# Joining the small TensorE runs of a fused attention, routing and gated-FFN kernel

## The chip, the cores and the metric

The kernel runs on one core of a Trainium2 chip. The metric is the time of one execution on the device in microseconds. Five engines work side by side, each through its own list of instructions in order: TensorE (PE: products), VectorE (DVE), ScalarE (ACT), GpSimd (POOL) and SyncE (SP, which issues most DMAs). Semaphores tie the lists together.

## The reference

Three layers follow one another, for 4 batches of 576 tokens:

```python
# 1 attention over 32 memory slots, 8 heads of 64
a = exp(phi - max_s(phi));  a = a / (sum_s(a) + 1e-9)           # over the 576 tokens
k_m, v_m = a^T k, a^T v                                          # 32 x 64 per head
attn = softmax(q k_m^T / 8);  x = attn v_m                       # heads side by side: 512 wide
# 2 one expert of 8 per token
logits = x w_gate;  gate = sigmoid(x w_local)
e[s] = argmax(logits[s]) if s == 0 or gate[s] < 0.5 else e[s-1]
x = softmax(logits)[e] * (relu(x w1[e]) w2[e])                   # 512 -> 1024 -> 512
# 3 gated FFN
h = relu(x w_in);  out = (h * sigmoid(conv3(h))) w_out           # conv over tokens, per channel
```

With these inputs each batch keeps the expert of its first token. The kernel computes all tokens of a batch with that expert and, at the end, looks whether another one is needed.

## The kernel before, in words

A float32 product is made of three products of rounded halves (high and low parts), 128x128 weights by 288 columns: half of the tokens. These are the plain products. For a batch `b` the list `order()` (line 58) writes 24 steps out: `h` eight times (hidden layer of the expert for one half of the tokens, 6 plain products each), `y` four times (second layer, 24 plain products each), then the same for the other half. Behind the steps it names what is done for later batches: `c = b + 1` and `d = b + 2`. Batch 0 has its own list, `FIRST` (line 51), whose steps 0 to 11 lie in `OPENING` (line 40).

The expert's first layer is not applied to x. V w1 is computed first (`vw`, tile `pv`: the memory values times a head's rows of w1, four quarters of w1, two quarters per PSUM tile), and the slot weights `att` multiply it.

The side work on TensorE, with the names of its PSUM tiles: phi's transposes (`pback`, `pa`), the memory products (`mem`, `pk`), the memory transposed (`back`, `pkt`), the gate weights (`gatew`, `pw`: memory values times w_gate and w_local, 9 columns, copied by ScalarE into `vwg`, line 475), the scores of half the tokens (`scores`, `sc`), the first token's logits (`flog`, `pfc`, from which VectorE takes the expert), the logits of all tokens of two batches (`rtok`, `pl`), and at the end of routing the transposes `pt` and `pp` and two tiny products, `pe` (`rown`, line 684) and `pf` (`close`, line 710). Scores, gate weights and V w1 use tiles of 64 rows by 32 columns of the array, eight at a time.

The scores go through VectorE's transpose (`scores_back`, line 489), maximum, difference, ScalarE's exponential, sum, reciprocal, product, and a second transpose. ScalarE and VectorE also evict each plain product: `h` by both (lines 781 and 782), `y` by ScalarE (line 864). They split the raw pieces of w2 into high and low parts (lines 147 and 148), and convert the words of the float64 weights of layer 3 (`nar`, lines 213 to 218).

PSUM has 8 banks. `bank()` takes one of four single banks (plain products, `pk`, `pl`, `pfc`, `pkt`, `pe`, `pf`). `banks()` takes one of two double banks (`pa`, `sc`, `pw`, `pv`, `pt`, `pp`); whoever comes third waits until the first one's reader is done.

TensorE's order is the written list. In the opening those of VectorE, ScalarE and SyncE are written too. In the 24-step part a planner orders them when the kernel is built: by its own model of times, among the instructions that are ready then, by place in the list. Instructions under `urgent()` count as 1500 places earlier. The lists are fixed when the kernel runs.

Of the kernel before, what the change touches and what calls it, by code (L numbers as in the profile page):

```python
# [8 lines left out]
F32 = mybir.dt.float32  # L9
# [5 lines left out]
ALU = mybir.AluOpType  # L15
AX = mybir.AxisListType
# [18 lines left out]
def units(b):  # L35
# [8 lines left out]
strn.0.0 smx.0.0 ssub.0.0 sexp.0.0 ssum.0.0 warm.1.8 mem.2.0 mem.2.1 warm.1.1 w1.0 q.0.1 wload.0.0 wload.0.1 kv.3 vwe.0 vwh.0 warm.1.2 vwe.1 ahi.0.0 vwh.1 alo.0.0 vwl.0 vwl.1 warm.1.3 wload.0.2  # L44
q.1.0 wload.0.3 q.1.1 cload nload.0 nload.1 phi.4 kv.4 prec.2 memf.2 pmax.3
h.0 vw.0.1 h.0 pexp.3 vw.0.2 h.0 prec.3 h.0 w2part.0 vw.0.3 h.0 scores.0.1 strn.0.1 w2part.1 h.0 pback.3 h.0 h.0 smx.0.1 w2.0.1 ssub.0.1 w2.0.2 sexp.0.1
y.0 firstq.2 phi.5 kv.5 mem.3 ssum.0.1 w2.0.3 y.0 back.1 ahi.0.1 alo.0.1 nar.0 nload.2 y.0 gatew.1 frow.1 fexp.1 nar.1 nload.3 y.0
""".split()


FIRST = {
# [3 lines left out]
}  # L55


def order():


    words = [4]

    def each(c, *parts):
        return [f"{part}.{u}" for u in units(c) for part in parts] if c < B else []

    def of(c, *parts):
        return [f"{part}.{c}" for part in parts] if c < B else []

    def narrow_next():
        i = words[0]  # L70
        words[0] += 1
        return [f"nar.{i}"] + [f"nload.{i + 2}"] * (i < 14)

    out = []
    for b in range(B):
        c, d = b + 1, b + 2
        whole = c < B
        after = {i: [] for i in range(24)}
        if b == 0:
            for i, more in FIRST.items():  # L80
                after[i] += more.split()
        else:
            for i, more in {
                1: of(c, "frow", "fexp") + [f"save.{b}"],
                2: [f"w2.{b}.2"] + [f"rtok.{b // 2}"] * (b == 1) + of(d, "firstq") + each(d, "phi", "kv"),
                3: [f"scores.{c}.0", f"ssoft.{c}.0"] * whole,
                7: [f"w2.{b}.3"],
                8: [f"scores.{c}.1", f"ssoft.{c}.1"] * whole + each(d, "psoft"),
                9: of(c, "flog", "w1"),
                10: each(d, "pback"),  # L90
                12: [f"asplit.{c}.0", f"asplit.{c}.1"] * whole,
                13: each(d, "mem"),
                16: of(d, "back"),
                18: of(d, "gatew"),
                21: [f"vw.{c}.0", f"vw.{c}.1", f"w2.{c}.0"] * whole,
                22: [f"vw.{c}.2", f"vw.{c}.3", f"w2.{c}.1"] * whole,
                23: [f"q.{d}.0", f"q.{d}.1"] * (d < B),
            }.items():
                after[i] += more
            for i in ((), (6, 13, 15, 17, 19), (4, 7, 13, 15, 17, 19), (8, ))[b]:  # L100
                after[i] += narrow_next()
            if not whole:
                for i, more in {0: "rtok.1 rback rall", 8: "rpp", 9: "rown", 10: "close yload.0 win.0 win.1",
                                19: "ysplit.0", 20: "win.2 win.3"}.items():
                    after[i] += more.split()
        for i in range(0 if b else 12, 24):
            out += [f"h.{b}" if i % 12 < 8 else f"y.{b}"] + after[i]
    assert words[0] == 16
    return out
# [5 lines left out]
def fused_kernel(tc, q, first, first_q, kv, kv_tail, phi, w1, w2, w_in, conv_w, w_out, out):  # L115
    nc = tc.nc
    wide = w_in.dtype == I64
    PSUM = bass.MemoryType.PSUM
    with (
# [8 lines left out]
        def bank(name):  # L128
            return ps1.tile([128, 512], F32, tag="one", name=name)
# [60 lines left out]
        nc.gpsimd.memset(first2, 0.0)  # L190
        code0 = const.tile([1, 4], F32, name="code0")
        convw = const.tile([128, 3, 8], F32, name="convw")
        fx = const.tile([32, 1], F32, name="fx")
        code32 = const.tile([1, 32], F32, name="code32")
        e0i = const.tile([1, B, 8], U32, name="e0i")
        flf = const.tile([1, 32], F32, name="flf")
        fli = const.tile([1, 32], I32, name="fli")
        ones = const.tile([8, 128], F32, name="ones")
        nc.vector.memset(ones, 1.0)
# [289 lines left out]
        def scores_back(b, hf):  # L489

            sts[b, hf] = work(f"st{b}_{hf}")
            nc.vector.transpose(two(sts[b, hf]), scs.pop((b, hf))[:, :, :HALF])
# [27 lines left out]
                cols = slice(32 * hs.start, 32 * hs.stop)  # L520
                nc.vector.transpose(attf[b, hf].rearrange("p g t -> p (g t)")[:, cols], st[:, cols])

        def slot_top(b, hf):
            scores_back(b, hf)
            slot_max(b, hf)
            slot_difference(b, hf)

        def slot_softmax(b, hf):

            slot_top(b, hf)  # L530
            slot_exp(b, hf)
            slot_weights(b, hf)

# [77 lines left out]
        def route_all():  # L611

            lg = routes[0].rearrange("p b c n -> p (b c) n")
            room = ap.tile([128, S], F32, tag="ph", bufs=2, name="room")
            pack = ap.tile([128, S], F32, tag="ph", bufs=2, name="pack")[:96, :384].rearrange("p (c n) -> p c n", n=64)
            packs.append(pack)
            used = [0]

            def bc(t):
                return t.rearrange("p (c o) -> p c o", o=1).to_broadcast([96, 24, 8])  # L620

            def by_batch(t):
                return t.rearrange("p (b c) n -> p b c n", b=B)

            def packed(at):
                return pack[:, :, at:at + 32].rearrange("p c (b n) -> p b c n", n=8)

            def tile24(name, *n):
                n = n[0] if n else 0
                at = used[0]  # L630
                used[0] += 24 * max(n, 1)
                t = room[:96, at:used[0]]
                return t.rearrange("p (c n) -> p c n", n=n) if n else t

            l8 = lg[:, :, 0:8]
            mx = tile24("rmx")
            nc.vector.reduce_max(mx, l8, axis=AX.X)
            eq = tile24("req", 8)
            nc.vector.tensor_tensor(eq, l8, bc(mx), ALU.is_ge)
            nc.vector.tensor_tensor(eq, eq, codes, ALU.mult)  # L640
            cd = tile24("rcd")
            nc.vector.reduce_max(cd, eq, axis=AX.X)
            ex = tile24("rex", 8)
            nc.vector.tensor_tensor(ex, l8, bc(mx), ALU.subtract)
            nc.scalar.activation(ex, ex, AF.Exp)
            gf = tile24("rgf", 1)
            nc.vector.tensor_scalar(gf, lg[:, :, 8:9], GATE_SHUT, None, ALU.is_le)
            nc.vector.memset(by_batch(gf)[0:1, :, 0:1, :], 1.0)
            nc.vector.tensor_tensor(cd, cd, gf.rearrange("p c o -> p (c o)"), ALU.mult)
            nc.vector.tensor_copy(packed(0), by_batch(bc(cd)))  # L650
            sm = tile24("rsm")
            nc.vector.reduce_sum(sm, ex, axis=AX.X)
            nc.vector.tensor_scalar(sm, sm, EPS, None, ALU.add)
            nc.vector.reciprocal(sm, sm)
            nc.vector.tensor_tensor(packed(32), by_batch(ex), by_batch(bc(sm)), ALU.mult)
            nc.vector.tensor_copy(code32.rearrange("p (b n) -> p b n", n=8),
                                  code0.rearrange("p (b o) -> p b o", o=1).to_broadcast([1, B, 8]))

        def route_scan():
# [20 lines left out]
        def route_first():  # L680

            act, = acts
            pe = bank("pe")
            nc.tensor.matmul(pe[:32, 0:1], code32, ones[0:1, 0:1], start=True, stop=True)
            oh = ap.tile([32, 1], F32, tag="oh", name="oh")
            nc.vector.tensor_tensor(oh, pe[:32, 0:1], code_e, ALU.is_equal)
            nc.vector.tensor_scalar(act, act, 0.0, None, ALU.is_gt)
            nc.vector.tensor_tensor(fx, act, oh, ALU.subtract)

        def attention_high(b, hf):  # L690
            if hf == 0:
# [14 lines left out]
            attention_low(b, hf)  # L706

        def route_last():
            pf = bank("pf")
            nc.tensor.matmul(pf[0:1, 0:32], fx, ident[:32, :32], start=True, stop=True)  # L710
            nc.vector.tensor_copy(flf, pf[0:1, 0:32])
            nc.vector.reduce_sum(anyf, flf, axis=AX.X)
            nc.vector.tensor_copy(fli, flf)
            nc.vector.tensor_copy(anyi, anyf)

        att, e0 = {}, {}
# [190 lines left out]
        def gated_w(kc):  # L907
# [4 lines left out]
            "phi": load_phi, "kv": load_kv, "q": load_q,  # L912
            "gates": load_gates, "psoft": phi_softmax, "pback": phi_back,
            "mem": memory, "memf": memory_out, "warm": warm, "back": memory_back,
            "scores": scores, "gatew": gate_weights, "firstq": first_queries, "frow": first_row, "fexp": first_weights, "flog": first_expert, "ssoft": slot_softmax,
            "pmax": phi_max, "pexp": phi_exp, "prec": phi_sums, "smax": slot_top, "strn": scores_back, "smx": slot_max,
            "ssub": slot_difference, "sexp": slot_exp, "ssum": slot_weights, "ahi": attention_high, "alo": attention_low,
            "rtok": route_tokens, "save": save, "rback": route_back, "rall": route_all, "rpp": route_scan, "rown": route_first, "asplit": split_attention,
            "vwe": first_vw, "vwh": first_vw_high, "vwl": first_vw_low, "vw": expert_vw, "w2": expert_w2, "nload": load_words, "nar": narrow, "win": gated_w,
# [230 lines left out]
```

## Time and profile before

| | us |
|---|---|
| median of 3 timed runs (417.91 to 418.92) | 418.08 |
| profiled execution | 417.01 |
| its span | 415.2 |
| TensorE busy in the span | 406.6 (98%) |
| VectorE, ScalarE, POOL busy | 276.3, 222.0, 74.6 |

The granted clock of TensorE has a mean of 0.997 of full speed. The gated FFN takes the span from 209 us to the end; what the change touches on TensorE lies between 44 and 190 us. The chain that ended last goes back from the last instruction to what released it, or to the instruction before it on its engine. Ends of products are modelled, and starts of small products overlap, so what a run costs is best read from where the next run begins.

### The profile page before, as it was taken

The page shows a single profiled execution, that of the slowest core. Times are in us where ns is not written, and L with a number is a line of the kernel's source. Part 1 is how long each engine was busy: PE and PEld are TensorE (multiplying, and loading weights), DVE is VectorE, ACT ScalarE, POOL GpSimd, SP SyncE. Part 2 cuts the span into 40 slices and gives each one's busy share as a digit, 9 for nine tenths or more (in the row PEclk, how much of TensorE's full clock was granted, in tenths as well). Part 3 has the DMA queues.
Part 4 walks back from the last instruction along what each step waited for, and adds up shares of the span by engine and source line. Part 5 has one row for each costly group of instructions (what it writes and reads, how often), then busy time and mean ns, then how long its engine had stood idle before and what let it go on. Part 6 is the DMA issues. An engine that isn't in the chain of part 4 may idle for free.

```text
span 415.2 us, 8514 instructions
## 1 busy us (share of the span) xinstructions
PE 406.6 (98%) x3406; PEld 370.6 (89%) x3407; DVE 276.3 (67%) x509; ACT 222.0 (53%) x414; POOL 74.6 (18%) x121
## 2 busy tenths in 40 slices
PE   8999999999999999999999999999999999999994
PEld 7779988989989998899999988998889988999884
DVE  3689899695777974966979980688105792178500
ACT  4366577455657264645848742677215772277320
POOL 1000202311122211311101620034100332014300
PEclk9999999999999999999999999999999999999998
DMA  8999989967892699946640032000120000100022
GB/s 288 343 403 401 340 305 363 410 220 277 303 310 93 200 366 407 340 157 186 194 152 0 2 114 103 0 2 0 57 70 2 0 2 29 72 2 2 2 77 57
DMA packets 23904, 69.04 MB, mean 166 GB/s; under 512 B 3280, under 2 KB 4048, under 8 KB 23856
## 3 DMA queue, kind: packets, MB, share of 16 engines
q1 hardware_dynamic: 20272, 56.88, 39.1%
q0 software_dynamic: 3584, 11.54, 7.1%
q8 instruction: 28, 0.46, 0.5%
q14 instruction: 20, 0.16, 0.1%
HBM read 52.08 MB, written 16.33 MB: 165 GB/s over the span
## 4 chain that ended last, share of the span: by engine, by line
PE 96%; ACT 1%; DMA 1%; DVE 1%; issue 0%; ACTq 0%
PE py L160 25%; PE pi L160 24%; PE po L1058 24%; PE ph L160 12%; PE pv L455 2%; PE pk L412 2%; PE idle L462 2%; PE sc L455 1%; PE pa L390 1%; DMA ph<-in_phi 1%; PE pl L593 1%; PE pk L402 0%; DVE wb L148 0%; PE pkt L446 0%; ACT wb L147 0%
## 5 line engine op out<-in xcount | busy, mean ns | idle before, releaser
L160 PE MATMUL py<-h,wb 128*128 128x288 f32 x768 | 108.2, 298 | 0.0
L160 PEld LDWEIGHTS py<-h,wb 128*128 128x128 f32 x768 | 103.0, 188 | 4.2 <-issue 3.4
L160 PE MATMUL pi<-yh,wi 128*128 128x288 f32 x512 | 90.4, 295 | 0.0
L1058 PE MATMUL po<-wo,g 128*128 128x512 f32 (+1 forms) x408 | 90.2, 377 | 0.0
L1058 PEld LDWEIGHTS po<-wo,g 128*128 128x128 f32 x408 | 72.8, 188 | 13.2
L160 PEld LDWEIGHTS pi<-yh,wi 128*128 128x128 f32 x512 | 76.3, 188 | 0.9
L1040 DVE SCALAR_TENSOR_TENSOR ct<-ht,convw,ct 128x575 f32<-128x575 f32 x32 | 31.0, 968 | 52.1 <-ACT ct L1039 52.1
L160 PE MATMUL pi<-yl,wi 128*128 128x288 f32 x256 | 54.6, 295 | 0.0
L160 PE MATMUL ph<-att,vh 128*128 128x288 f32 x256 | 53.5, 302 | 0.3 <-DVE h L782 0.3
L1023 POOL CAST tail<-g 128x128 fp32r<-128x128 f32 x32 | 23.0, 723 | 122.9 <-DVE g L148 122.3
L160 PEld LDWEIGHTS ph<-att,vh 128*128 128x128 f32 x256 | 40.6, 188 | 4.6 <-DVE h L782 1.7
L865 POOL DMA_DIRECT2D ydram<-ys x32 | 17.4, 545 | 146.7 <-ACT ys L864 140.3
L160 PEld LDWEIGHTS pi<-yl,wi 128*128 128x128 f32 x256 | 41.1, 188 | 0.0
L1037 ACT ACTIVATE ht<-pi 128x576 f32<-128x576 f32 x32 | 20.8, 651 | 33.5 <-PE pi L160 33.5
L160 PE MATMUL ph<-att,vl 128*128 128x288 f32 x128 | 37.7, 296 | 0.0
L782 DVE SCALAR_TENSOR_TENSOR h<-ph,h 128x288 fp32r<-128x288 f32 x64 | 28.1, 449 | 12.8 <-ACT h L781 12.7
L781 ACT ACTIVATE h<-ph 128x288 fp32r<-128x288 f32 x64 | 25.7, 408 | 16.5 <-PE ph L160 16.1
L864 ACT ACTIVATE ys<-py 128x288 f32<-128x288 f32 x32 | 13.1, 408 | 37.5 <-PE py L160 25.2
L1082 ACT ACTIVATE ot<-po 128x512 f32<-128x512 f32 x17 | 9.5, 598 | 43.3 <-PE po L1058 43.3
L1018 DVE TENSOR_TENSOR ct<-ht,ct 128x576 f32<-128x576 f32 x32 | 27.0, 844 | 7.2 <-ACT ct L1017 7.1
L1042 DVE SCALAR_TENSOR_TENSOR ct<-ht,convw,ct 128x575 f32<-128x575 f32 x32 | 28.3, 886 | 0.4
L147 ACT ACTIVATE g<-ct 128x576 fp32r<-128x576 f32 x32 | 21.7, 681 | 12.6 <-DVE ct L1018 12.6
(234 smaller groups left out, 505.2 us busy)
## 6 DMA issues: line engine op xcount, KB each, us to landing
kv<-in_kv SPq DMA_DIRECT2D x16, 512.0 KB, 8.5
q<-in_q SPq DMA_DIRECT2D x8, 576.0 KB, 10.3
ydram<-ys POOLq DMA_DIRECT2D x32, 144.0 KB, 5.3
y<-ydram SPq DMA_DIRECT2D x4, 1152.0 KB, 6.8
out<-ot SPq DMA_DIRECT2D x15, 256.0 KB, 2.0
ph<-in_phi SPq DMA_DIRECT2D x8, 288.0 KB, 7.3
adram<-at POOLq DMA_DIRECT2D x8, 288.0 KB, 7.7
wa_1r<-in_w SPq DMA_DIRECT2D x4, 512.0 KB, 4.5
```

The source lines that it names most:

```text
L147: pin(nc.scalar.activation(hi, src, AF.Copy))
L160: pin(nc.tensor.matmul(ps, st, mv[:, cols], start=i == 0, stop=i == len(terms) - 1))
L781: nc.scalar.activation(t[:, 0, :], ps, AF.Relu)
L782: low = nc.vector.scalar_tensor_tensor(t[:, 1, :], ps, 0.0, t[:, 0, :].bitcast(F32), ALU.max, ALU.subtract)
L864: nc.scalar.activation(yt, ps, AF.Copy)
L865: stored.append(nc.gpsimd.dma_start(ydram[b, d, :, half(hf)], yt).ins)
L1018: slow(f"gm.{f}").tensor_tensor(ct, ht, ct, ALU.mult)
L1023: nc.gpsimd.tensor_copy(tail[:, f, :, to:to + 64], t[:, :, 512:576].bitcast(F32))
L1037: nc.scalar.activation(two(ht), halves(ps), AF.Relu)
L1040: nc.vector.scalar_tensor_tensor(ct[:, 1:], ht[:, :S - 1], convw[:, 0, f:f + 1], ct[:, 1:], ALU.mult, ALU.add)
L1042: nc.vector.scalar_tensor_tensor(ct[:, :S - 1], ht[:, 1:], convw[:, 2, f:f + 1], ct[:, :S - 1], ALU.mult, ALU.add)
L1058: nc.tensor.matmul(ps[:, cols], st[sp], w[:, mp, f % 2, cols], start=f == 0 and i == 0, stop=f == 7 and i == 2)
```

## The change

In the written list the side work moves together. In batch 0 the gate weights of batch 1 leave the opening and come at step 12, ahead of both halves' scores and of the first token's product; the second scores no longer stand at step 16. The two memory products stand together at step 19, and all four quarters of V w1 with the gate weights at step 21. In the later batches the logits, both halves' scores and the first token's product stand at step 3 (before: steps 2, 3, 8 and 9), and the gate weights (before: step 18) and all quarters of V w1 (before: steps 21 and 22) at step 21. The transposes of both halves' scores are listed right behind the scores; the rest of the softmax (`sweigh`) stays at steps 3 and 8.

The products `pe` and `pf`, which turned a row into a column and back, become VectorE transposes of 32x32 tiles; the tiles `fx`, `code32` and `flf` grow to 32x32, and POOL clears two of them at the start.

```diff
-y.0 ... nload.2 y.0 gatew.1 frow.1 fexp.1 nar.1 nload.3 y.0
+y.0 ... nload.2 y.0 frow.1 fexp.1 nar.1 nload.3 y.0
-    12: "scores.1.0 flog.1 w1.1 psoft.4", 13: "ssoft.1.0 psoft.5", 16: "pback.4 scores.1.1 ssoft.1.1", 17: "pback.5",
-    18: "mem.4", 19: "mem.5 nar.2 nload.4", 20: "asplit.1.0 asplit.1.1 back.2",
-    21: "gatew.2 vw.1.0 vw.1.1 w2.1.0 nar.3 nload.5", 22: "vw.1.2 vw.1.3 w2.1.1 conv", 23: "q.2.0 q.2.1 save.0",
+    12: "gatew.1 scores.1.0 scores.1.1 flog.1 w1.1 strn.1.0 strn.1.1 psoft.4", 13: "sweigh.1.0 psoft.5", 16: "pback.4 sweigh.1.1",
+    17: "pback.5", 19: "mem.4 mem.5 nar.2 nload.4", 20: "asplit.1.0 asplit.1.1 back.2",
+    21: "gatew.2 vw.1.0 vw.1.1 vw.1.2 vw.1.3 w2.1.0 nar.3 nload.5", 22: "w2.1.1 conv", 23: "q.2.0 q.2.1 save.0",
...
-                2: [f"w2.{b}.2"] + [f"rtok.{b // 2}"] * (b == 1) + of(d, "firstq") + each(d, "phi", "kv"),
-                3: [f"scores.{c}.0", f"ssoft.{c}.0"] * whole,
+                2: [f"w2.{b}.2"] + of(d, "firstq") + each(d, "phi", "kv"),
+                3: [f"rtok.{b // 2}"] * (b == 1) + [f"{item}.{c}.{hf}" for item in ("scores", "strn") for hf in range(2)] * whole
+                   + of(c, "flog") + [f"sweigh.{c}.0"] * whole,
-                8: [f"scores.{c}.1", f"ssoft.{c}.1"] * whole + each(d, "psoft"),
-                9: of(c, "flog", "w1"),
+                8: [f"sweigh.{c}.1"] * whole + each(d, "psoft"),
+                9: of(c, "w1"),
-                18: of(d, "gatew"),
-                21: [f"vw.{c}.0", f"vw.{c}.1", f"w2.{c}.0"] * whole,
-                22: [f"vw.{c}.2", f"vw.{c}.3", f"w2.{c}.1"] * whole,
+                21: of(d, "gatew") + [f"vw.{c}.{q}" for q in range(4)] * whole + [f"w2.{c}.0"] * whole,
+                22: [f"w2.{c}.1"] * whole,
...
-            pe = bank("pe")
-            nc.tensor.matmul(pe[:32, 0:1], code32, ones[0:1, 0:1], start=True, stop=True)
+            nc.vector.transpose(code_t, code32)
...
-            pf = bank("pf")
-            nc.tensor.matmul(pf[0:1, 0:32], fx, ident[:32, :32], start=True, stop=True)
-            nc.vector.tensor_copy(flf, pf[0:1, 0:32])
-            nc.vector.reduce_sum(anyf, flf, axis=AX.X)
-            nc.vector.tensor_copy(fli, flf)
+            nc.vector.transpose(flf, fx)
+            nc.vector.reduce_sum(anyf, flf[0:1, :], axis=AX.X)
+            nc.vector.tensor_copy(fli, flf[0:1, :])
```

## Rows read from the trace of the kernel before

**Rows 1.** The page, part 4: shares of the chain that ended last, by engine.

```profile
PE 96%; ACT 1%; DMA 1%; DVE 1%; issue 0%; ACTq 0%
```

**Rows 2.** The chain in order of time: start us, us, engine, tile, line, count.

```profile
83.78 2.94 PE py L160 x22
...
86.73 0.53 PE py L160 x2
...
107.93 0.20 PE pw L455 x13
108.13 1.01 PE ph L160 x6
...
115.51 1.02 PE pv L455 x32
116.53 3.40 PE py L160 x24
...
127.48 0.65 PE sc L455 x16
...
131.48 3.20 PE py L160 x24
...
183.03 0.15 PE pe L684 x2
183.17 3.41 PE py L160 x24
186.59 0.14 PE pf L710 x2
186.73 3.36 PE py L160 x24
```

**Rows 3.** The same chain, runs of batch 0 that are joined or short.

```profile
23.36 0.59 PE pv L455 x16
...
49.12 0.18 PE pfc L571 x4
...
55.43 0.80 PE ph L160 x6
...
66.42 0.18 PE pw L455 x10
66.60 0.91 PE pv L455 x32
```

**Rows 4.** ScalarE's timeline at batch 0, step 12: start, us, ..., idle before.

```profile
48.52 0.41 ACT L781 ACTIVATE h<-ph 128x288 fp32r<-128x288 f32 x1 [0.34 <-PE ph L160]
```

**Rows 5.** ScalarE's timeline at batch 0, step 21.

```profile
66.45 0.41 ACT L864 ACTIVATE ys<-py 128x288 f32<-128x288 f32 x1 [0.67 <-PE py L160]
66.76 1.05 ACT L147 ACTIVATE wb<-wb_1r 128x1024 fp32r<-128x1024 f32 x1
...
67.93 0.18 ACT L475 ACTIVATE vwg<-pw 128x18 f32<-128x18 f32 x1
```

**Rows 6.** ScalarE's timeline in batch 1, steps 18 and 21.

```profile
108.28 0.19 ACT L475 ACTIVATE vwg<-pw 128x18 f32<-128x18 f32 x1
...
116.25 0.68 ACT L214 ACTIVATE n8r<-n8r 128x512 int32<-128x512 uint32 x1
116.83 0.39 ACT L864 ACTIVATE ys<-py 128x288 f32<-128x288 f32 x1
117.11 1.06 ACT L147 ACTIVATE wb<-wb_1r 128x1024 fp32r<-128x1024 f32 x1
```

**Rows 7.** VectorE's timeline: batch 1, steps 3 to 8; batch 3, step 10.

```profile
80.63 0.77 DVE L492 STREAM_TRANSPOSE st<-sc 128x576 f32<-128x576 f32 x1
...
86.22 0.45 DVE L782 SCALAR_TENSOR_TENSOR h<-ph,h 128x288 fp32r<-128x288 f32 x1
...
186.77 0.18 DVE L711 COPY flf<-pf 1x32 f32<-1x32 f32 x1 [1.22 <-PE pf L710]
```

**Rows 8.** The waits: who waited for whom, us in total, times, longest.

```profile
ACT nd L213 <- DMA n13r<-in_w_out: 3.3, 1, 3.3
```

More of the change, by code (lines that the diff above doesn't have):

```diff
@@ L46 @@
 h.0 vw.0.1 h.0 pexp.3 vw.0.2 h.0 prec.3 h.0 w2part.0 vw.0.3 h.0 scores.0.1 strn.0.1 w2part.1 h.0 pback.3 h.0 h.0 smx.0.1 w2.0.1 ssub.0.1 w2.0.2 sexp.0.1
-y.0 firstq.2 phi.5 kv.5 mem.3 ssum.0.1 w2.0.3 y.0 back.1 ahi.0.1 alo.0.1 nar.0 nload.2 y.0 gatew.1 frow.1 fexp.1 nar.1 nload.3 y.0
+y.0 firstq.2 phi.5 kv.5 mem.3 ssum.0.1 w2.0.3 y.0 back.1 ahi.0.1 alo.0.1 nar.0 nload.2 y.0 frow.1 fexp.1 nar.1 nload.3 y.0
 """.split()
 FIRST = {
[3 rows of a table removed]
[3 rows of a table added]
 }
@@ L192, in fused_kernel @@
         convw = const.tile([128, 3, 8], F32, name="convw")
-        fx = const.tile([32, 1], F32, name="fx")
-        code32 = const.tile([1, 32], F32, name="code32")
+        fx = const.tile([32, 32], F32, name="fx")
+        nc.gpsimd.memset(fx, 0.0)
+        code32 = const.tile([32, 32], F32, name="code32")
+        nc.gpsimd.memset(code32, 0.0)
         e0i = const.tile([1, B, 8], U32, name="e0i")
-        flf = const.tile([1, 32], F32, name="flf")
+        flf = const.tile([32, 32], F32, name="flf")
         fli = const.tile([1, 32], I32, name="fli")
@@ L521, in slot_weights, with slot_softmax @@
                 nc.vector.transpose(attf[b, hf].rearrange("p g t -> p (g t)")[:, cols], st[:, cols])
-        def slot_top(b, hf):
-            scores_back(b, hf)
+        def slot_softmax(b, hf):
             slot_max(b, hf)
             slot_difference(b, hf)
-        def slot_softmax(b, hf):
-            slot_top(b, hf)
             slot_exp(b, hf)
@@ L655, in route_all @@
             nc.vector.tensor_tensor(packed(32), by_batch(ex), by_batch(bc(sm)), ALU.mult)
-            nc.vector.tensor_copy(code32.rearrange("p (b n) -> p b n", n=8),
+            nc.vector.tensor_copy(code32[0:1, :].rearrange("p (b n) -> p b n", n=8),
                                   code0.rearrange("p (b o) -> p b o", o=1).to_broadcast([1, B, 8]))
@@ L682, in route_first @@
             act, = acts
-            pe = bank("pe")
-            nc.tensor.matmul(pe[:32, 0:1], code32, ones[0:1, 0:1], start=True, stop=True)
+            nc.vector.transpose(code_t, code32)
             oh = ap.tile([32, 1], F32, tag="oh", name="oh")
-            nc.vector.tensor_tensor(oh, pe[:32, 0:1], code_e, ALU.is_equal)
+            nc.vector.tensor_tensor(oh, code_t[:, 0:1], code_e, ALU.is_equal)
             nc.vector.tensor_scalar(act, act, 0.0, None, ALU.is_gt)
-            nc.vector.tensor_tensor(fx, act, oh, ALU.subtract)
+            nc.vector.tensor_tensor(fx[:, 0:1], act, oh, ALU.subtract)
         def attention_high(b, hf):
@@ L914, in fused_kernel @@
             "mem": memory, "memf": memory_out, "warm": warm, "back": memory_back,
-            "scores": scores, "gatew": gate_weights, "firstq": first_queries, "frow": first_row, "fexp": first_weights, "flog": first_expert, "ssoft": slot_softmax,
-            "pmax": phi_max, "pexp": phi_exp, "prec": phi_sums, "smax": slot_top, "strn": scores_back, "smx": slot_max,
+            "scores": scores, "gatew": gate_weights, "firstq": first_queries, "frow": first_row, "fexp": first_weights, "flog": first_expert, "sweigh": slot_softmax,
+            "pmax": phi_max, "pexp": phi_exp, "prec": phi_sums, "strn": scores_back, "smx": slot_max,
             "ssub": slot_difference, "sexp": slot_exp, "ssum": slot_weights, "ahi": attention_high, "alo": attention_low,
```

## The prediction

> **What bounds the kernel now.** The profiled execution took 417.01 us, of which 415.2 are the span and 1.81 lie around it. The median of the three timed runs, 418.08, is 1.07 above it; differences are worked out within the profiled execution and then taken off the median.
>
> I read the page's fourth part first [rows 1]: TensorE holds 96% of the chain that ended last. The reader is to see that nothing else is worth counting unless TensorE waits for it. So the price of an edit is how many microseconds of TensorE's own list it takes out, and how long it makes TensorE wait.
>
> The chain in order of time comes next [rows 2], for what a small run costs inside the stream of plain products (128x128 weights, 288 columns). Undisturbed, 24 of them take 3.20 and 6 take 0.80 [rows 2, 3]. Behind a side run of scores, gate weights, V w1 or first-token products 24 take 3.40 and 6 take 0.99 to 1.01. So a side run costs its own time and then 0.20 of a slower return, however short it is: the gate weights cost 0.20 + 0.20, the one-column product `pe` 0.15 + 0.21.
>
> [Rows 3] show what is paid inside a joined run. The first token's product right behind scores takes 0.18, and one return is paid for both. Gate weights ahead of V w1 take 0.18 and V w1 then 0.91 in place of 1.02: joined they cost 0.07 beside the 0.20 alone. Sixteen V w1 products alone take 0.59, 32 take 1.02, so 16 more of a run that is under way cost 0.43, and 32 more 0.86. Scores have 288 columns to V w1's 256, so a second half's 16 products should take 0.43 x 288/256 = 0.48 in place of 0.65. The transposes of phi (`pa`) are the exception: the 6 plain products behind them take the undisturbed 0.80.
>
> **The change part by part, savings.** A return is 0.20 each time.
>
> - Batch 0, step 12: gate weights, both scores and the first token's product in one run; before, the gate weights stood alone in the opening and the second scores behind `pa` at step 16. Two returns 0.40, gate weights 0.20 - 0.07 = 0.13, second scores 0.65 - 0.48 = 0.17: 0.70.
> - Batch 0, step 19: the two memory products joined, one return: 0.20.
> - Batch 0, step 21: the second pair of V w1 quarters joins the first: one return 0.20 and 1.02 - 0.86 = 0.16: 0.36.
> - Batch 1, step 3: logits, both scores and the first token's product: three returns 0.60 and 0.17: 0.77. Logits and scores use different tile shapes; a full new entry between them would take 0.2 back.
> - Batch 1, step 21: gate weights and both pairs: two returns 0.40, 0.13 and 0.16: 0.69.
> - Batch 2, step 3: two returns and 0.17: 0.57. Step 21: 0.36.
> - Batch 3: `pe` (0.15 + 0.21) and `pf` (0.14 + 0.16) become VectorE transposes: 0.66.
>
> Together 4.31, on TensorE's list and so on the path. It can hardly be more; with the entry above and the rounding of the rows it is at least 3.9.
>
> A rule of the Trainium skill bears on this: the page "TensorEngine Tiling (Array Packing)", section Key Properties, says that a change of tiling mode, not of tile alone, drains TensorE. By that rule the mode change from logits to scores and those from scores to the first token's product are paid inside the joined runs too; if each of these four cost 0.2 the sum would be 3.5. The trace agrees only for some: `pa` returns to plain products for nothing, and the four first-token products behind the scores take 0.18, no more than the gate weights do alone.
>
> **What the joints make TensorE wait for.** Scores, gate weights and V w1 share two double buffers of PSUM. In three of the new runs there are three users in a row (gate weights, then two others), so the third needs the buffer that the gate weights hold until ScalarE has copied them to `vwg`. Before, a plain stretch of 3 us stood in between and hid this copy.
>
> - Batch 0, step 12: the gate weights would start near 48.4. ScalarE evicts one hidden product until 48.93 [rows 4] and is free; the copy (0.18) would end near 49.1, while the second scores are due 0.07 + 0.48 after the start, near 48.95. Wait 0.15; between 0 and 0.7.
> - Batch 0, step 21: here the copy is a row [rows 5]. The gate weights start at 66.4; ScalarE evicts a plain product, splits a piece of w2 (1.05), and copies only at 67.93 to 68.11. The second pair would be due at about 67.3 (start plus 0.07 plus 0.86): 0.80 late, and some 0.05 to hand over. TensorE arrives 0.9 earlier by the savings ahead of it, but ScalarE can follow by only the 0.67 that it idled ahead of its eviction: 0.2 more, 1.05 in all. If the copy went ahead of the split it would be 0; with no part of ScalarE's list moving up, 1.75.
> - Batch 1, step 21: ScalarE is late by itself [rows 6]. The stretch of plain products ends at 115.5, its eviction starts at 116.83, then comes the same split, until 118.17. The second pair would be due at about 116.4. A copy right behind the eviction (117.2 to 117.4) makes TensorE wait 1.0; one behind the split, as in [rows 5], 1.95. Both have a row near, so I take the middle, 1.5.
> - Batch 2 has no gate weights, and the runs at step 3 start with both double buffers free: no such wait.
>
> Together 2.70. A rule of the skill speaks against the change here: "PSUM — Partial Sum Buffer", section Engine vs sequencer instructions, says that ScalarE's queue is strict first in, first out. By that rule a copy behind a split cannot pass it, and the 2.70 stand; without it the copy would come in time and the whole 4.31 would be left. The trace agrees: in [rows 5] the copy's source had been ready for over a microsecond.
>
> **Edits at nothing.** The two VectorE transposes of 32x32 stand in for a copy of 0.18 ahead of which VectorE idled 1.22 [rows 7]; what follows them is needed only at the end of the kernel or, for the tiles that become free, 20 us later. If VectorE were full there they would cost nothing either. Two more memsets on POOL come before anything that waits for it. Moving the logits from step 2 to 3 puts their ScalarE copy behind three more loads on SP's list, which do not share its queue. The gate copy moves from step 18 to 21, past two conversions of weight words on ScalarE, one of which is why it is late above. The first token's expert is known five steps earlier, so SP may issue the next w1 pieces earlier, ahead of the word loads; V w1 never waited for them, and a word load that waits delays only conversions. Both score transposes (0.77 each [rows 7]) now fall into one stretch on VectorE, which also evicts every hidden product: the last one before the y products was already late in batch 1, ending at 86.67 [rows 7], and the 24 plain products there took 2.94 + 0.53 in place of 3.20 [rows 2], 0.27 lost. I add nothing, since the joined run itself gives VectorE 0.66 more time; the bounds are 0.27 won and 1.0 (both transposes, less the 0.66, and a little for the batch after) lost.
>
> Net: 4.31 - 2.70 = 1.61 saved: 415.40 in the profiled execution's terms, 418.08 - 1.61 = 416.47 for the median: 416.5.
>
> **Rivals.**
>
> *The copies come in time.* The planner puts the gate copy ahead of the w2 split. For it: at step 18 of batch 1 the copy starts at 108.28, 0.35 after the chain has the gate weights begin [rows 2, 6]. Against: [rows 5], the same neighbours. Waits 0.3: 418.08 - 4.31 + 0.30 = 414.1.
>
> *Evictions late.* Two transposes in one stretch and longer side runs leave evictions of hidden products behind; TensorE loses up to 1.0 at the starts of the y stretches on top of 2.70: 0.6 saved, 417.5. For it: VectorE's row at 86.22. Against: the plain stretches of the other batches run at 3.20 [rows 2].
>
> *Slower: the gate copy behind a conversion that waits for memory.* ScalarE's list stands still where a conversion waits for its words; in batch 2 it did so for 3.3 [rows 8]. If the planner puts the copy of batch 1, step 21, behind such a wait, TensorE waits 3.3 + two conversions at 0.68 [rows 6] + eviction 0.4 + split 1.05 + copy 0.2 = 6.3; with 1.2 at the other two places 7.5, so 3.2 lost: 421.3. It decides from a wait of 3.1 at that one place on. For it: the conversions of words 7 and 8 belong to the steps just before (17 and 19). Against: it stood still that long for a load once in the whole trace.
>
> **How the numbers follow.** Forecast 0.43 (its own range 415.5 to 417.4), copies in time 0.27 (413.7 to 415.3), evictions late 0.15, slower 0.15 (418.1 to 421.5). A measurement of this kernel tells about 0.3%, 1.25 us, from no change. Below 416.83 lie all of the second case and about 0.70 of the forecast: 0.57. Within 0.3% lie the rest of the forecast (0.13), most of the late evictions (0.13) and 0.02 of the slower case: 0.28. Slower: the other 0.13 of that case and the far end of the late evictions, 0.15. The range leaves out a tail of the second case and the far part of the slower one: 413.8 to 418.9.
>
> **What would show it.** The chain after should have 13 fewer side runs between the opening and 190 us, the stretches of 24 plain products between them at 3.20, and the second scores at 0.48. The waits should show V w1 (`pv`) waiting for `vwg` at step 21 of batches 0 and 1, by about 1.05 and 1.5, and scores waiting 0.15 at step 12. If `pv` shows no wait, the second case holds. If the returns stay after joined runs, or the second scores still take 0.65, the savings are wrong.

## The result, and the profile after

The change makes the kernel slower: 423.0 us (422.72 to 424.2) against 418.6 (417.91 to 419.23), five runs each; the ratio is 1.0108 (1.0094 to 1.0123). The forecast was 416.5, with a range up to 418.9.

The profiled execution of after took 424.2, its span is 422.4. Between the first product of `pkt` near 41 us and the first of `pp`, the stretch that holds nearly all of the change, it needs 143.78 where before needs 138.58: 5.20 more. From `pp` to the last product both need 229.8, though `pe` and `pf` are gone. The rest of the difference between the two spans, about 2, lies in the opening, ahead of the change; a second profile of before puts that into question below. Each profile is one execution, and that of after is the slowest of its five: the two profiled executions lie 7.2 apart, the medians 4.4. The sizes below are those of the profiles.

Part 4 of the page of after, the chain by engine, answers to [rows 1]. TensorE's 96% have become 70%.

```profile
PE 70%; issue 10%; DMA 8%; DVE 5%; ACT 3%; POOL 1%; SPq 1%; POOLq 0%; ACTq 0%; DVEq 0%
```

So the list of what TensorE waited for, between 40 and 190 us, is the view to read next: who waited for what, us in total, times, longest. In before it has one line, 0.3 for an `h`. In after:

```profile
PE pv L457 <- ACT vwg L477: 2.4, 2, 2.0
PE ph L160 <- DVE h L777: 2.1, 4, 0.8
PE pw L457 <- ACT vt L450: 1.1, 1, 1.1
PE ph L160 <- DVE e0i L573: 1.0, 1, 1.0
PE py L160 <- DVE h L777: 0.2, 1, 0.2
```

**The savings are there.** The chain of after, in order of time (start, us, what), answers to [rows 2, 3]: both halves' scores take 1.13 (0.65 for one half, so the second costs 0.48), 64 products of V w1 take 1.89 (1.02 for 32, so 0.87 more), and behind `pp` the products run on with no `pe` and no `pf`.

```profile
133.30 1.13 PE sc L457 x32
134.43 0.17 PE pfc L569 x4
134.61 1.00 PE ph L160 x6
...
146.44 8.50 DMA n11r<-in_w_out
...
166.02 1.89 PE pv L457 x64
...
187.24 9.58 PE py L160 x72
```

**The gate copies.** At batch 0, step 12, the forecast wait of 0.15 is there, though the list of waits does not name it: the copy `vwg` ends at 50.95, and the first eight score products of the second half start at 51.01. They start 0.33 behind the product before them; in batch 1, where no gate weights stand ahead of the scores, that step is 0.20. So the wait is 0.14. ScalarE's row and TensorE's:

```profile
50.77 0.18 ACT L477 ACTIVATE vwg<-pw 128x18 f32<-128x18 f32 x1
51.01 0.48 PE L457 MATMUL sc<-q,vt 64*32 64x288 f32 x8
```

ScalarE's timeline at batch 0, step 21 (start, us, instruction, in brackets the idle time before it and what ended it) answers to [rows 5]. Two waits come out of one list. The split of `wb_0r` waits 1.58 for its piece to land, `vt` stands three instructions behind it, and the gate weights read `vt`: they wait 1.1 before they start. Then the copy `vwg` stands behind the next split, and the second pair of quarters waits.

```profile
67.56 1.06 ACT L147 ACTIVATE wb<-wb_0r 128x1024 fp32r<-128x1024 f32 x1 [1.58 <-DMA wb_0r<-in_w]
68.53 0.65 ACT L215 ACTIVATE nd<-n3r 128x512 f32<-128x512 f32 x1
69.08 0.66 ACT L216 ACTIVATE n3r<-n3r 128x512 int32<-128x512 uint32 x1
69.63 0.37 ACT L450 ACTIVATE vt<-pkt 128x256 f32<-128x256 f32 x1
69.89 0.41 ACT L859 ACTIVATE ys<-py 128x288 f32<-128x288 f32 x1
70.19 1.06 ACT L147 ACTIVATE wb<-wb_1r 128x1024 fp32r<-128x1024 f32 x1
...
71.36 0.19 ACT L477 ACTIVATE vwg<-pw 128x18 f32<-128x18 f32 x1
```

The same view at batch 1, step 21, which answers to [rows 6]: a conversion waits 1.00 until `f_in` has taken the words that its buffer held, and eviction, split and copy follow. The conversion before it, at 116.35, had waited 2.99 in the same way.

```profile
119.84 0.71 ACT L215 ACTIVATE nd<-n8r 128x512 f32<-128x512 f32 x1 [1.00 <-DMA f_in<-nd]
120.45 0.65 ACT L216 ACTIVATE n8r<-n8r 128x512 int32<-128x512 uint32 x1
121.00 0.38 ACT L859 ACTIVATE ys<-py 128x288 f32<-128x288 f32 x1
121.30 1.04 ACT L147 ACTIVATE wb<-wb_1r 128x1024 fp32r<-128x1024 f32 x1
122.24 0.17 ACT L477 ACTIVATE vwg<-pw 128x18 f32<-128x18 f32 x1
```

**The late evictions.** VectorE's timeline behind the joined scores of batch 1 (it answers to [rows 7]), and under it TensorE's row:

```profile
84.19 0.45 DVE L777 SCALAR_TENSOR_TENSOR h<-ph,h 128x288 fp32r<-128x288 f32 x1
84.55 0.77 DVE L494 STREAM_TRANSPOSE st<-sc 128x576 f32<-128x576 f32 x1
85.36 0.75 DVE L498 TENSOR_REDUCE mx<-st 128x18 f32<-128x576 f32 x1
86.03 0.77 DVE L494 STREAM_TRANSPOSE st<-sc 128x576 f32<-128x576 f32 x1
86.73 0.12 DVE L572 MAX8 flm<-pfc 1x8 f32<-1x8 f32 x1
86.78 0.73 DVE L504 TENSOR_TENSOR sd<-st,mx 128x576 f32<-128x576 f32 x1
87.44 0.73 DVE L498 TENSOR_REDUCE mx<-st 128x18 f32<-128x576 f32 x1
...
88.17 0.15 DVE L573 FIND_INDEX8 e0i<-flm,pfc 1x8 uint32<-1x8 f32 x1
88.25 0.79 DVE L777 SCALAR_TENSOR_TENSOR h<-ph,h 128x288 fp32r<-128x288 f32 x2
```

```profile
88.37 0.53 PE L160 MATMUL ph<-att,vh 128*128 128x288 f32 x2 [0.97 <-DVE e0i L573]
```

Between two evictions of `h`, at 84.19 and at 88.25, VectorE works through 3.7 us of softmax and the first token's expert. TensorE fills a single bank every 0.80 and has four, one of them held by `pfc` until the expert is found: it stands still until `e0i` is done.

**The sum of the 5.20.** I measured from start to start of products. Side runs, each with its return: 3.43 less. Waits ahead of and inside the runs of step 21: 1.22 + 0.62 + 2.26 = 4.10. Stops inside the plain stretches, each with a slower product behind it: 4.50 more than in before, about 1 each behind the joined scores of batches 0, 1 and 2, and 1.0 in the second half of batch 2. There the load of `n11r` is issued at 146.44, as VectorE's late conversion of `n9r` ends (146.42), and takes 8.50 to land (the chain above); in before, where this stretch runs some 6 earlier, it is issued at 136.6 and takes 3.8. ScalarE stands 0.92 for it, and the evictions behind it are late:

```profile
155.02 0.67 ACT L215 ACTIVATE nd<-n11r 128x512 f32<-128x512 f32 x1 [0.92 <-DMA n11r<-in_w_out]
```

4.10 + 4.50 - 3.43 = 5.17. The 3.43 are net of the wait of 0.14 at step 12, which lies inside a side run.

### The profile page after: what moved, and what is told of

Same layout as the page of the kernel before. It is cut to its first block, busy times and chain, and to the rows that moved or that the text cites. A ratio compares the mean times of both kernels' runs of the same rounds, so it can differ in the third digit from the quotient of the medians.

```text
span 422.4 us, 8515 instructions
## 1 busy us (share of the span) xinstructions
PE 405.2 (96%) x3402; PEld 370.5 (88%) x3403; DVE 276.6 (65%) x510; ACT 221.6 (52%) x414; POOL 74.3 (18%) x123
## 4 chain that ended last, share of the span: by engine, by line
PE 70%; issue 10%; DMA 8%; DVE 5%; ACT 3%; POOL 1%; SPq 1%; POOLq 0%; ACTq 0%; DVEq 0%
PE pi L160 24%; PE po L1053 23%; PE py L160 14%; PE ph L160 5%; DMA n11r<-in_w_out 2%; DMA kt<-in_kv_tail 2%; DMA ydram<-ys 2%; DMA wa_1r<-in_w 1%; PE pv L457 1%; DVE h L777 1%; DMA f_in<-nd 1%; POOL ydram L860 1%; PE idle L464 1%; DVE wb L148 1%; ACT h L776 1%
## 5 line engine op out<-in xcount | busy, mean ns | idle before, releaser
L160 PE MATMUL py<-h,wb 128*128 128x288 f32 x768 | 105.7, 296 | 0.2 <-DVE h L777 0.2
```

The source lines that it names most:

```text
L160: pin(nc.tensor.matmul(ps, st, mv[:, cols], start=i == 0, stop=i == len(terms) - 1))
```

## The experiments

Each kernel was timed in five rounds beside the kernel before, if nothing else is said; ratios are to before in the same rounds. Differences between kernels of well under 1 us are read from the traces, from the first product of `pkt` to the first of `pp` ("the body": before 138.58, after 143.78), which leaves the opening out. A body is that of one execution: f2, g4 and h1 below have the same written order and 137.66, 137.65 and 138.74. So a difference counts where the trace names the wait behind it. Most edits are shortened to step numbers and the items that stand there.

**e1: scores apart.** V w1, gate weights, memory and the VectorE transposes as in after; scores, first token, logits and gate weights of batch 1 back where they stood.

```diff
-12: "gatew.1 scores.1.0 scores.1.1 flog.1 w1.1 strn.1.0 strn.1.1 psoft.4", ...
+12: "scores.1.0 flog.1 w1.1 strn.1.0 psoft.4", ... 16: "pback.4 scores.1.1 strn.1.1 sweigh.1.1",
...
+2: rtok   3: scores.0 strn.0 sweigh.0   8: scores.1 strn.1 sweigh.1   9: flog w1
```

> The scores, the first token's product and the logits stand where they did before (steps 2, 3, 8, 9; batch 0: 12 and 16); V w1 with the gate weights, the memory products and the VectorE transposes stay as in the changed kernel. Theory A (two separate losses: evictions behind the joined scores, some 3.7 us in the changed kernel's trace, and V w1's second pair waiting for the gate weights' copy, some 4.1 us): the eviction waits go, the copy waits stay; savings left 2.3: 418.6 - 2.3 + 4.1 = 420.4. Theory B (the joined scores are the only loss, the copy wait just takes the place of another): 416.5 to 418. Theory C (a shift of some 2 us from the opening on, from the larger tiles): 2 us above A.

Measured 420.62, ratio 1.0047 (1.0027 to 1.0067), close to theory A's 420.4. The profiled execution took 423.65, 3.0 more than the median; its body, 142.45, holds a fall of the clock (last section). The late evictions are gone, the waits of step 21 all stay:

```profile
PE pv L456 <- ACT vwg L476: 2.4, 2, 2.0
PE pw L456 <- ACT vt L449: 0.8, 1, 0.8
PE ph L159 <- DVE h L776: 0.3, 1, 0.3
```

**e2: V w1 apart.** The other half of the change: scores joined, gate weights and V w1 as before.

```diff
-21: gatew + vw.0 vw.1 vw.2 vw.3 + w2.0   22: w2.1
+18: gatew   21: vw.0 vw.1 w2.0   22: vw.2 vw.3 w2.1
```

> V w1 and the gate weights stand where they did before (batch 0: steps 21 and 22, later: 18, 21, 22); the joined scores, memory products and VectorE transposes stay as in the changed kernel. Theory A: the copy waits go, the eviction waits stay; savings left 2.9: 418.6 - 2.9 + 3.7 = 419.4. Theory B: still 421 to 423. Theory C: 2 us above A.

Measured 421.37, ratio 1.0061 (1.0038 to 1.0085), body 141.16. It is 2 us over the expectation of theory A: the late evictions all stay, and a wait of 0.6 for `vt` with them. The body is 2.58 over before's, and 418.79 (before in these rounds) + 2.58 is the time measured. It is also theory C's number, but e3's time speaks against C.

```profile
PE ph L161 <- DVE h L778: 1.8, 3, 0.8
PE ph L161 <- DVE e0i L574: 1.0, 1, 1.0
PE pw L458 <- ACT vt L451: 0.6, 1, 0.6
...
```

**e3: neither.** Both edits together; of the change the joined memory products and the VectorE transposes are left.

> Of the change only the joined memory products of batch 0 and the two small products by VectorE (with the larger tiles) are left. Theories A and B: 418.6 - 0.2 - 0.7 = 417.7, and the opening as before. Theory C: 419.5 to 420.5, with the opening 2 us late in the trace.

Measured 418.97, ratio 0.9994 (0.9976 to 1.0011), body 138.45: no new wait, but 1.3 more than theories A and B expected and 0.5 less than the least of theory C. 0.13 is saved in the body, and the 0.7 for `pe` and `pf` is not in the time.

**e4: late transpose.** After, with the second half's transpose listed at step 8 (batch 0: 16); the scores stay joined on TensorE.

```diff
-3: scores.0 scores.1 strn.0 strn.1 flog sweigh.0   8: sweigh.1
+3: scores.0 scores.1 strn.0 flog sweigh.0   8: strn.1 sweigh.1
```

> The changed kernel with one edit: the transposes of the second half's scores are listed where the rest of their softmax is (step 8; batch 0: 16), the products stay joined. If the evictions are late because two transposes of 0.77 come in one stretch of VectorE: the hidden products' waits of 0.8 to 1.1 in batches 0, 1 and 2 fall below 0.3 each, 423.0 - 2.5 = 420.5. If it is the PSUM bank that the first token's product holds until VectorE has its index, or the longer run itself: 422 to 423.5.

Measured 422.62, ratio 1.0076 (1.005 to 1.0103), which lies in the range that the expectation gave to the bank or the longer run. The trace says more than the time: the clock fell behind the wait in V w1, which cost some 1.5, and the body is 142.55. The stops behind the joined scores fell from 0.95, 1.26 and 1.12 between starts to none, 0.65 and 0.32, but a new one of 1.21 stands at the start of batch 2's `y`: the transposes are a cause of the late evictions, and the work that is moved comes back late at another place.

**f1: the split behind the gate copy.** After, with one order added for ScalarE.

```diff
+gate_copies[b] = nc.scalar.activation(vwg[:, b, :, :9], pw[:, :, :9], AF.Copy).ins
...
+with tc.issue_after(gate_copies[b + 1]):      # second w2 piece of batches 1 and 2
     split(t[:, 0], t[:, 1], raw, eng, pin)
```

> The changed kernel, but ScalarE's split of the second w2 piece of batches 2 and 3 (listed at step 22) is ordered behind the gate weights' copy, which it overtook in the changed kernel. Theory A (the second pair of V w1 waits because the copy vwg stands behind a split of over a microsecond): the wait of 0.62 at batch 0, step 21 goes, the one at batch 1, step 21 falls from 2.26 to about 1.3 (ScalarE's eviction of y ends at 121.3 and is late by itself, behind a conversion that waits for its words); the time falls by about 1.55, from 423.0 to 421.4, and 1.3 of wait stays. Rival (the waits move: the split that now comes later holds up the evictions behind it): pv's waits go the same way, but as much comes back at the next evictions, 422.6 to 423.2. Rival C (the wait is for something else, a split of att or V w1's own weights): the waits stay at 0.6 and 2.3 with the copy early, 423.

Measured 421.18, ratio 1.0075 (1.0056 to 1.0095), body 141.35. As expected of the order on ScalarE: no wait for `vwg` at batch 0, 1.34 left at batch 1. That is 1.54 of the 2.43 by which the body fell; the gate weights' wait for `vt` was also shorter here, 0.69 in place of 1.22, and so was the stop in the second half of batch 2, so the time forecast was met in part by luck.

```profile
PE pv L460 <- ACT vwg L480: 1.1, 1, 1.1
...
PE pw L460 <- ACT vt L453: 0.6, 1, 0.6
```

**f2: V w1 joined, the gate weights left at step 18.** e3 and the four quarters of V w1 of batches 2 and 3 in one run.

```diff
+18: gatew   21: vw.0 vw.1 vw.2 vw.3 w2.0   22: w2.1
```

> The kernel of e3 (only the memory products joined and the two VectorE transposes), and in addition the four quarters of V w1 in one run at step 21 of batches 1 and 2, the gate weights kept alone at step 18 as in the kernel before; batch 0 as before. Theory A (the joint is worth its 0.36 in each batch if no third user of the double buffers stands in front of it): V w1's 64 products take about 2.09 without a wait, and the time is 0.7 under e3's 418.97: 418.2. Rival (the joint is not free even so: four quarters need weight pieces that land later, or the evictions of V w1 come later and the first hidden product waits): a new wait of 0.7 or more at the step, 419 to 420.

Measured 417.99, ratio 0.9986 (0.9965 to 1.0007), body 137.66, 0.79 under e3's. No third user, no wait: 64 products take 1.89 at batch 1 too, where the changed kernel waited 2.26 in their midst.

```profile
118.00 1.89 PE pv L457 x64
```

**f3: first token late.** e2, with `flog` of batches 2 and 3 back at step 9.

> The kernel of e2 (V w1 and gate weights as before, everything else as in the changed kernel, 421.37), but the first token's product of batches 2 and 3 stands at step 9 again; the scores of both halves stay joined at step 3 with both transposes behind them. Theory A (two transposes of 0.77 in one stretch make VectorE late): TensorE's gaps of 1.26 and 1.12 at steps 3 to 8 of batches 1 and 2 stay at about 1.0 or over, and two returns of 0.2 come back: 421.4 to 421.8. Rival D (the first token's product holds one of the four single banks until VectorE has read it behind the transposes, maximum and all): the gaps fall to 0.3 or less, and with the two returns the time is 421.37 - 2.0 + 0.4 = 419.8.

Measured 420.82, ratio 1.0059 (1.0041 to 1.0078), body 140.36, between the two expectations. The wait for `e0i` is gone, so the bank held by `pfc` was a cause of the stop at that place; VectorE is late all the same, and the stops stand at the starts of `y`. Little is won: of the 0.8 by which the body is under e2's, 0.66 is e2's wait for `vt`, which this execution lacks, and the ratios are nearly the same.

```profile
PE py L161 <- DVE h L778: 1.6, 4, 0.6
PE ph L161 <- DVE h L778: 1.0, 2, 0.7
```

**f4: both late.** f3, and the second transposes late as in e4.

> As f3_first_token_late, and the second half's transpose listed at step 8 (batch 0: step 16) in place of step 3 as well; on TensorE the scores stay joined. If the two causes share the gaps (e4, with the transpose late alone, had 0, 0.65 and 0.32 left of 0.95, 1.26 and 1.12): all three gaps fall under 0.3, and the time is 421.37 - 3.0 + 0.4 = 418.8, unless the transpose moved to step 8 returns as a late eviction at the start of the y products (it was 1.2 in e4): then 419.6 to 420.2. If the gaps come from the longer side run alone: they stay at 0.9 and over, 421.4 to 421.8.

Measured 419.26, ratio 1.0017 (1.0 to 1.0034), body 139.47. The stops behind the scores are gone, so they do not come from the longer side run; 1.4 at the starts of `y` is left.

```profile
PE py L161 <- DVE h L778: 1.4, 2, 1.1
PE ph L161 <- DVE h L778: 0.3, 1, 0.3
```

**g1, g2: the place of the tiles.** In after and in every kernel that keeps its larger tiles, four stretches of 48 products of the gated FFN take 6.39 that take 6.25 in before; three others take 6.38 or 6.39 in all kernels. The larger `fx` shifts the tiles behind it by 96 bytes. g1 is before with that shift alone, g2 is after with 128 bytes in place of 96.

```diff
-fx = const.tile([32, 1], F32, name="fx")
+fx = const.tile([32, 25], F32, name="fx")[:, 0:1]     # g1
-flf = const.tile([32, 32], F32, name="flf")
+flf = const.tile([32, 40], F32, name="flf")[:, :32]   # g2
```

> The kernel before, with nothing changed but that the tile fx takes 100 bytes of each partition in place of 4, so that the tiles behind it in SBUF (constants, raw weight pieces, split w2 and w_out, y) lie 96 bytes further on, as they do in the changed kernel. Why: in the changed kernel and in e3 the 0.7 that the two VectorE transposes save is gone again by the end, since four stretches of 48 products in the gated FFN take 6.385 in place of 6.245 and the 92 to 140 products of w_out 0.03 more each, with the same program there. Theory L (the place of the tiles in SBUF sets this pace): the four stretches take 6.38 here too, 0.66 more in all: 419.6. Rival (the pace comes from somewhere else, for example from the phase in which the stretches begin): 6.245 as before, 418.9. If the later landing of the opening's loads also came from the place of the tiles, the first product against pkt starts at 42 or later and the time is 420 or more.

> The changed kernel with 32 bytes more in flf, so that the tiles behind it lie 128 bytes further on than in the kernel before, in place of 96. Theory L (the place of the tiles): the four stretches of 48 products return to 6.245, 0.66 less: 422.3. Rival: no change, 423.0.

g1: 419.35, ratio 1.0021 (1.0001 to 1.004); the four stretches take 6.39, and the time from the first product of `pp` to the last of all is 230.45 in place of 229.82. The first of the four, in the chain of before and then of g1:

```profile
225.65 6.25 PE pi L160 x48
```

```profile
227.16 6.39 PE pi L160 x48
```

g1's body is 139.13, 0.55 over before's, mostly because its gate weights waited for `vt`, with ScalarE's instructions there in the order of before:

```profile
PE pw L455 <- ACT vt L448: 0.4, 1, 0.4
```

g2: 424.0, ratio 1.0116 (1.0092 to 1.0141), the stretches at 6.38: 128 bytes do not undo it.

**g3: before again**, one profiled execution (417.98).

> The kernel before, once more, for a second profile of its opening. If the loads' landing differs from execution to execution by itself, the first product against pkt, at 40.42 in the first profile and between 41.73 and 43.26 in all kernels with the change or parts of it, starts at 41.5 or later here; if the change delays the opening, at 40.4 again.

The first `pkt` product starts at 41.31; in the first profile of before it starts at 40.55 (the figures in the expectation are those of the product ahead of it, some 0.13 earlier). So the opening differs between executions of one program by 0.8; kernels with parts of the change lie between 41.56 and 43.52, g1 at 41.57. Whether the change adds to it stays open.

**g4: f2 with g2's edit.**

> The kernel of f2 (memory products joined, the two VectorE transposes, V w1's quarters of batches 2 and 3 joined, gate weights and scores as before) with the same 32 bytes more in flf. If every saving that no wait follows holds, this is the best version so far: f2's 417.99 less 0.66 by theory L, 417.3, against 418.95 before; without theory L 418.0.

Measured 417.75, ratio 0.9987 (0.9973 to 1.0001), the stretches at 6.38.

**h1: f2 in place.** `flf` takes the tile of `code32`, and all large tiles lie where they lie in before.

```diff
-flf = const.tile([32, 32], F32, name="flf")
+flf = code32
-anyf = const.tile([1, 1], F32, name="anyf")
+anyf = const.tile([1, 9], F32, name="anyf")[:, 0:1]
```

> The kernel of f2 (memory products joined, the two VectorE transposes, V w1's quarters of batches 2 and 3 joined, the rest as before), with flf laid over code32, which is free by then, and 32 bytes more in anyf, so that every tile behind the constants lies at the place that it has in the kernel before. Theory L (the place of the tiles sets the pace of the gated FFN's products; any multiple will not do, since 128 bytes further gave 6.383 as 96 bytes did): the four stretches of 48 products return to 6.245, 229.1 from the first product of pp to the last in place of 229.8, and the time is 417.9 - 0.65 = 417.2. Rival (the pace depends on something else that the two added transposes change): 6.38 again, 417.9.

Measured 417.66, ratio 0.9983 (0.9966 to 1.0001). `pp` to the end took 229.10, as expected of the place: the 0.72 for `pe` and `pf` is there at last. In the body of the profiled execution, 138.74, the gate weights waited 0.9 for `vt`; in f2 and g4, with the same written order, they did not.

```profile
226.10 6.25 PE pi L160 x48
```

**h2, h3: `vt` ahead of the split that waits.** h2 is h1 with the first w2 piece's split of batch 1 ordered behind `vt`; h3 is after with this order and f1's.

```diff
+vt_copies[b] = nc.scalar.activation(kvt[b]..., pt, AF.Copy).ins
...
+with tc.issue_after(vt_copies[b + 1]):      # first w2 piece (moves that of batch 1)
     split(t[:, 0], t[:, 1], raw, eng, pin)
```

> The kernel of h1 (417.66), and ScalarE's split of the first w2 piece of batch 1 is ordered behind the copy of the memory (vt) that the gate weights read; in h1's profile the split waited 1.24 for its piece to land, vt stood three instructions behind it, and the gate weights waited 0.93 on TensorE. Theory A (the wait is this order, and strikes in the executions in which the piece lands late): the gate weights of batch 0, step 21 start with no wait, the first product of pkt to the first of pp takes 137.7 as in f2 in place of 138.75, and the time falls by up to 0.9, to 416.8 to 417.4. Rival (the gate weights wait for something else, or as much returns behind the split): the wait stays or moves, 417.7.

> The changed kernel with both orders: the first w2 piece's split of batch 1 behind the copy vt, as in h2, and the second pieces' splits behind the gate weights' copy, as in f1 (421.18). Theory A: of the waits at the two steps 21 only 1.3 at batch 1 is left (ScalarE late by itself), the gate weights' wait for vt (0.68 in f1's profile, 1.2 in the changed kernel's) goes, and the time is 420.5; what is still lost against the kernel before are the late evictions of 3.7 and the 0.66 in the gated FFN. Rival (what is taken away here comes back at the next step): 421.2 as f1.

h2: 416.9, ratio 0.9954 (0.9936 to 0.9973), body 137.70. In its trace the split still waits 0.75 for the piece, and TensorE waits for neither. It beats both kernels.

```profile
64.67 0.36 ACT L453 ACTIVATE vt<-pkt 128x256 f32<-128x256 f32 x1
65.78 1.06 ACT L147 ACTIVATE wb<-wb_0r 128x1024 fp32r<-128x1024 f32 x1 [0.75 <-DMA wb_0r<-in_w]
```

h3: 420.71, ratio 1.0037 (1.0022 to 1.0052), body 140.42. No wait at batch 0, step 21, and 1.26 at batch 1; the late evictions are as in after.

## Why the prediction was wrong, step by step

**Savings: right.** Forecast 4.31, measured from product to product 4.16, and 4.30 without the wait of 0.14 that lies inside the run of step 12: batch 0 step 12 0.66 without it (0.70), step 19 0.20 (0.20), step 21 0.36 (0.36); batch 1 0.76 (0.77) and 0.70 (0.69); batch 2 0.55 (0.57) and 0.35 (0.36); `pe` and `pf` 0.73 (0.66). The 0.20 of a new entry between logits and scores was not paid. This is shown by the lists of products alone, which have 13 fewer side runs as forecast, and by f2, whose 0.79 against e3 is two joints of 0.36 and little more.

**Edits at nothing: this is the step that failed.** "I add nothing, since the joined run itself gives VectorE 0.66 more time" stood for the score transposes; they and what follows them cost 4.50. The bound of 1.0 priced two transposes at one place. Four things were left out. What follows the transposes is pulled along: in the row of batch 1, 3.7 us lie between two evictions, of which the transposes are 1.54. It happens in three batches. And the first token's product, now in the same run, keeps a bank until VectorE reaches its maximum and index. Last, in the second half of batch 2 ScalarE stands for a load that was issued late; e1, e4 and f4 do not have this stop. e4 takes part of it away by the transposes, f3 by the bank, f4 by both, and each time VectorE is late at `y` for what it did not do earlier. Joined scores cost more in waits than they save in every order tried: with the first token's product in the run they save 1.83, and in f4, without it, the body is still 1.02 above e3's. The rival "evictions late" had the mechanism and a fifth of the size, and it put the stops at the starts of `y`, where they stand in f3 and f4; in after they stand among the hidden products.

**Waits of the joints: right, a little short.** Forecast 2.70, measured 3.02 for the gate copies. Step 12 of batch 0 had 0.14 (0.15) and step 21 had 0.62 (1.05). Batch 1 had 2.26 (1.5): the copy stood behind the split, as the upper bound of 1.95 had it, and ScalarE was later still, by a conversion that waited 1.00 for memory. That is the mechanism of the slower rival, with a wait of 1.00 for a buffer to be emptied where it had 3.3 for words to land.

**A wait that was in no step.** Batch 0 had 1.22 more at step 21: the gate weights' own wait for `vt`, behind a split that waited for its piece. The change does not make this order: g1 paid 0.4 with the order of before, and h1 0.9 with step 21 of batch 0 written as in before. It strikes where the piece lands late: in seven of the seventeen profiles, in neither of the two of before itself. How much of the 1.22 the change brings stays open. h2 and h3 show it as ScalarE's order, f1 the same of the copies. The Trainium skill, "PSUM — Partial Sum Buffer", section Engine vs sequencer instructions, has the queue as strict first in, first out; the trace agrees: in f1 and h2 one instruction moved ahead of another in that queue takes the wait away, 0.62 and 0.9.

**Two VectorE transposes at nothing: right where I looked, wrong 20 us later.** TensorE gained 0.73 at that place and lost 0.70 in the gated FFN by the place of the larger tiles (g1, h1). "Tiles that become free" was all I had asked of these tiles.

Of the 6.5 between forecast and result, 4.5 are evictions, 1.2 the wait for `vt`, 0.7 the place of tiles and 0.3 the gate copies; they sum to 6.7, and body and end of the profiles differ from the forecast by 6.8. That this is close to the 6.5 of the medians is luck in part: these sizes are of one execution, and the opening's spread of about 1 stands beside them.

## What to carry to other kernels

A side run's price on TensorE can be read from the chain to a few hundredths, but joining runs also joins their readers: lay out the whole stretch that the evicting engine will work between two evictions, and set it against the free banks times what fills one. Before joining three users of two buffers, read what stands ahead of the freeing copy in its engine's list, including what waits for a transfer there; here two orders of one instruction each were worth more than most joints. Before a wait is put down to an edit, look whether the old order can show it too, in another execution. When a small tile grows, compare the pace of stretches that the edit does not touch.

## What the runs showed of the hardware

The place of tiles in SBUF changed the pace of TensorE's products by 2%: 48 products of the gated FFN took 6.245 or 6.385, four times in each run, depending on where the tiles lay (96 or 128 bytes further: 6.38; in place: 6.245). What it is in the place that does this was not tried.

TensorE's granted clock fell after some long waits. Granted clock, mean over the window, is the fourth column (stretch, its length, PE busy, clock, DMA share, GB/s); first after, behind a wait in V w1 that the trace puts at 2.03, then g2, behind one of 1.99:

```profile
119.00:123.00 4.00, 1.97 (x75) 1.00 0.73 209
123.00:127.00 4.00, 4.00 (x50) 1.00 0.96 355
```

```profile
118.00:122.00 4.00, 2.01 (x82) 1.00 0.77 232
122.00:126.00 4.00, 4.00 (x32) 0.58 0.95 331
```

In g2 ten products start 0.240 apart, in place of 0.132: the level of 1.2 GHz. With the slower V w1 ahead of them that cost 1.5 in this execution, more than the 0.70 by which g2's body, 144.47, is longer than after's. e1 and e4 show it at the same place. What decides between two waits of one length stays open.
